# Weights from float64 by integer shifts and one integer addition, on VectorE, with the first batch's square sums

## The chip, the cores and the metric

The kernel runs on one core of one Trainium2 chip. A core has TensorE (PE: products, with a weight load PEld ahead of each), VectorE (DVE), ScalarE (ACT), GpSimd (POOL) and SyncE (SP, which issues the DMAs here). The metric is device time in microseconds of one execution, median over the timed runs.

## The reference

Channel attention over 6080 tokens of 256 channels, for four batches, then a gated two-layer product over all 24320 tokens:

```python
qn = q / (norm(q, axis=1) + 1e-06);  kn = k / (norm(k, axis=1) + 1e-06)
s = kn.transpose(0, 2, 1) @ qn / tau          # 4 x 256 x 256
a = softmax(s, axis=-1)
x = (v @ a).reshape(24320, 256)
h = x @ w_in                                  # 256 x 2048
out = (h * (1 / (1 + exp(-1.702 * h)))) @ w_out   # 2048 x 256
```

q, k and v are float32. The two weights come as float64 and have to be rounded to float32 on the chip, which has no float64 arithmetic: each word arrives as two 32-bit halves, low (`lw`) and high (`hw`).

## The kernel before

v (a w_in) is computed in place of (v a) w_in: a w_in is 256 x 2048 and is made once per batch (`weights`, L370, in four groups of 512 columns). float32 operands are split into two parts, hi by ScalarE (`split`, L78) and lo = x - hi by a subtraction on VectorE (L79), and a product is three products of parts.

The first batch's attention runs alone (L465 to L521), in an order written out by hand. Units of two tiles of 128 tokens pass through it: q and k are loaded four tiles at a time, ScalarE squares them (L238), and the squares are summed into `acc_q` and `acc_k` (L241), while TensorE makes the scores from the raw float32 words (L257), five units behind. There are 25 units; the last two are shorter. Of these sums GpSimd takes those of q in every second unit, as far as the last six units, and VectorE all others. After the last unit, both sums are folded (L287), and `norms_a` takes the norms: TensorE's products with ones (L288) give `ps_n`, VectorE copies it, and GpSimd takes the square root as a power (L296). `norms_b` makes reciprocals and a diagonal on VectorE, `norms_c` the product `ps_b` (L311) and its copy (L316), `softmax_a` and `softmax_c` the rows x (L329 to L347), `transposes` ends it. The scores of the last three units and some products of no use (`keep_warm`, L463) stand between these on TensorE.

The tokens then come in chunks of 512. For each chunk and each of 16 blocks of hidden units, a step: six products into `ps_h` (`hidden`, L419), a sigmoid on ScalarE (L425), the product g on VectorE (L426, one input from PSUM), its split into gh and gl, and two steps later six products into `ps_o` (`project`, L444). `ps_h` has three buffers. The first two chunks of the first batch alternate, so that each block of hidden units is needed every second step only. From L540 on, the order of each engine's instructions is chosen by a scheduler that keeps the program's dependences.

The weights are converted in 16 pieces of 128x512 words by `to_float32`: two while q and k come in (units 10 and 14, `spread` false), the others beside the first 24 steps (the table at L528), each begun at its step and carried on in the two that follow. A piece is loaded (`words`), ScalarE makes the absolute value of the high half into z (L119) and the low half times 2^-52 into m (L121), VectorE clamps z (L125), shifts it (L127), puts the sign back (L130) and cuts out the exponent (L134); GpSimd multiplies `low` with m (L136) and adds (L143). With `spread` false VectorE makes L124 and L138 in place of ScalarE's and GpSimd's parts. Pieces of w_in end in `win`, which is split group by group (`win_h`, `win_l`); pieces of w_out are split at once, `wo_h` by ScalarE, `wo_l` by GpSimd. z, `low` and the words of w_out have two buffers each.

The other three batches' attention goes in between the tokens of the batch ahead of it, with its square sums on GpSimd (`prepare`); the first begins at step 34.

Of the kernel before, what the change touches and what calls it, by code (L numbers as in the profile page):

```python
# [19 lines left out]
# high words of 2^128 and of 2^-127 in float64, their bits read as float32  # L20
F64_TOP = float(np.array([1151 << 20], np.uint32).view(np.float32)[0])
F64_BOTTOM = float(np.array([896 << 20], np.uint32).view(np.float32)[0])
NCH = 512  # tokens of one chunk
FG = 4  # blocks of 128 hidden units in one group of the first product's weights
# [3 lines left out]
def channel_attention_then_glu(  # L28
# [10 lines left out]
    """out = act((v a) w_in) w_out, with a = softmax(kn^T qn / tau) of one batch.  # L39

    (v a) w_in is taken as v (a w_in): a w_in is 256 x 2048 and made once per batch.
    float32 operands of products are split into two float32r parts, x = hi + lo
    exactly (12 significant bits each); hi hi + hi lo + lo hi leaves out only what
    lies below float32's own rounding of a product.

    The weights come as float64, of which the chip has no arithmetic: as their bits.
    They are rounded to float32 here.
    """
# [3 lines left out]
    NC2 = C // P  # halves of the channels  # L52
# [5 lines left out]
    T = N // P  # whole tiles of 128 tokens  # L58
    TAIL = N - T * P
    UT = 2  # tiles of one unit of the scores' loop  # L60
    RT = 4  # tiles of one load
# [15 lines left out]
    def split(dst_hi, dst_lo, src, eng=nc.vector):  # L77
        ins = nc.scalar.copy(dst_hi, src)  # L78
        eng.tensor_tensor(dst_lo, src, dst_hi.bitcast(F32), op=ALU.subtract)  # L79
        return ins  # L80

# [23 lines left out]
    def to_float32(out, raw, shape, spread):  # L105
        """float64 to float32: 2^e (1 + 20 bits of the high word), and below it the low
        word times 2^(e - 52), in one rounded sum. The high word without its sign is
        clamped to float32's exponents first, as a float32 itself, in which order its
        bits stand: what is too small comes out within 2^-126, too large as inf or NaN.
        spread: ScalarE and GpSimd take what they can of it. In parts, one for  # L110
        ScalarE, two for VectorE, one for GpSimd; it gives the result's tile."""
        lw = raw[..., 0]
        hw = raw[..., 1]
        z = cv.tile(shape, U32, tag="z", name="z")
        zf = z.bitcast(F32)
        low = cv.tile(shape, U32, tag="low", name="low")
        lf = low.bitcast(F32)
        if spread:
            nc.scalar.activation(zf, hw.bitcast(F32), AF.Abs)  # L119
            m = sp.tile(shape, F32, tag="sq", name="m", bufs=4)  # L120
            nc.scalar.activation(m, lw, AF.Copy, scale=2.0**-52)  # L121
        yield
        if not spread:
            nc.vector.tensor_single_scalar(z, hw, 0x7FFFFFFF, op=ALU.bitwise_and)  # L124
        nc.vector.tensor_scalar(zf, zf, F64_TOP, F64_BOTTOM, op0=ALU.min, op1=ALU.max)  # L125
        # exponent e - 896 in eight bits: the first of e's bits, then its last seven
        nc.vector.tensor_scalar(  # L127
            z, z, 5, 2, op0=ALU.logical_shift_left, op1=ALU.logical_shift_right
        )
        nc.vector.scalar_tensor_tensor(  # L130
            z, in0=hw, scalar=0xC0000000, in1=z, op0=ALU.bitwise_and, op1=ALU.bitwise_or
        )
        yield
        nc.vector.tensor_single_scalar(low, z, 0xFF800000, op=ALU.bitwise_and)  # L134
        if spread:
            nc.gpsimd.tensor_tensor(lf, lf, m, op=ALU.mult)  # L136
        else:
            nc.vector.scalar_tensor_tensor(  # L138
                lf, in0=lw, scalar=2.0**-52, in1=lf, op0=ALU.mult, op1=ALU.mult
            )  # L140
        yield
        out = zf if out is None else out
        nc.gpsimd.tensor_tensor(out, zf, lf, op=ALU.add)  # L143
        return out
# [3 lines left out]
    def win_fetch(n):  # L148
        """A block of 128 rows and GW columns; the words wait in the room of the next
        batch's q and k."""  # L150
        g, c = divmod(n, NC2)
        gs = slice(2 * g * GW, 2 * (g + 1) * GW)
        src = w_in[c * P : (c + 1) * P, gs].rearrange("p (f w) -> p f w", w=2)
        words["in", n] = load_words(src, [P, GW], sp, ("raw_q", "raw_k")[c])

    def win_convert(n, spread=True):
        g, c = divmod(n, NC2)
        out = win[:, c, g * GW : (g + 1) * GW]
        yield from to_float32(out, words.pop(("in", n)), [P, GW], spread)

    def wout_fetch(u):
        """Two blocks of 128 rows."""
# [4 lines left out]
    def wout_convert(u):  # L167
        t = yield from to_float32(None, words.pop(("out", u)), [P, 2, C], True)
        yield
        fs = slice(2 * u, 2 * u + 2)  # L170
        split(wo_h[:, fs, :], wo_l[:, fs, :], t, nc.gpsimd)
# [5 lines left out]
    class Attention:  # L177
        def __init__(self, b, direct=False):
            self.b = b
            # direct: float32 products, four passes each, with nothing to be split  # L180
            self.direct = direct
            self.raw = {}
            # tiles of each load: a short one first
# [3 lines left out]
            # (first tile, tiles, partitions) of each unit  # L187
# [4 lines left out]
        def load(self, t0, room):  # L192
            """Tiles t0 .. of q and k; a partition's rows are contiguous in DRAM."""
            b = self.b
            nt = min(room, T - t0)
            # the very first tiles come one by one
            cuts = range(nt + 1) if self.direct and t0 == 0 else (0, nt)
            tiles = {}
            for a, z in zip(cuts, cuts[1:]):
                for src, tag in ((q, "raw_q"), (k, "raw_k")):  # L200
                    if tag not in tiles:
                        if self.direct:  # the room of weights that are not there yet
# [14 lines left out]
        def prepare(self, u):  # L217
# [6 lines left out]
            else:  # L224
                # [hi | lo] side by side, so that one product takes both parts of q
# [4 lines left out]
            for r, nm in ((rq, "acc_q"), (rk, "acc_k")):  # L230
# [4 lines left out]
                else:  # L235
# [3 lines left out]
                    fast = self.direct and (nm == "acc_k" or u % 2 or u >= len(self.units) - 6)  # L239
                    eng = nc.vector if fast else nc.gpsimd  # L240
# [38 lines left out]
        def norms_a(self):  # L279
            """Columns: norms of both halves of q's channels, then of k's."""  # L280
# [26 lines left out]
        def norms_c(self):  # L307
            """1 / (q's norms) along the free axis, on all partitions."""
# [9 lines left out]
        def softmax_a(self):  # L318
# [19 lines left out]
            # the table of the function that follows comes in while the vector engine works  # L338
# [31 lines left out]
        def weights(self, g, i):  # L370
            """Half i of group g of a w_in."""
# [62 lines left out]
    def project(b, c, f, gh, gl):  # L434
        o, w = chunks[c]
        if f == 0:
            # the second chunk of all runs beside the first, in the room of the scores
# [20 lines left out]
    def keep_warm(rhs, n):  # L458
        """Products of no use, where the tensor engine would wait long enough for its
        clock to be halved: the next ones would run at half the rate."""  # L460
# [11 lines left out]
    with tc.manual_schedule():  # L472
        keep_warm(ones, 8)
        parts = []
        for u in range(nu):
# [7 lines left out]
            if u in early:  # L483
                parts.append(win_convert(early[u], False))
                next(parts[-1])
                next(parts[-1])
# [40 lines left out]
    # the weights' conversions, each begun at its step  # L527
# [116 lines left out]
```

## Time and profile before

| | |
|---|---|
| time, median of 3 runs | 2319.41 us (2319.32 to 2321.55) |
| span of the profiled execution | 2318.9 us |
| TensorE (PE) busy | 2295.2 us, 99%, 10300 records |
| VectorE (DVE) busy | 1397.3 us, 60% |
| ScalarE (ACT) busy | 1221.7 us, 53% |
| GpSimd (POOL) busy | 281.8 us, 12%, 207 records |

The times further below are us from the span's start, of the one profiled execution. The page gives no time of that execution beside its span. The shares are means over the whole span; the start of the kernel looks otherwise, and the rows below are of it. PEclk is the clock that TensorE was granted, as a share of 2.4 GHz. A record of an engine can begin before the one ahead of it has ended, by some 0.08 us on VectorE.

### The profile page before, as it was taken

How to read it: one execution, taken by the hardware profiler on the slowest of the kernel's cores; microseconds unless marked ns; L12 is line 12 of the kernel's file. 1: busy time of each engine (PE TensorE's matmuls, PEld its weight loads, DVE VectorE, ACT ScalarE, POOL GpSimd, SP SyncE). 2: the span in 40 equal slices, each digit the busy share in tenths (PEclk: the TensorE clock that was granted, in tenths of full speed). 3: DMA queues.
4: the chain of work that ended last, by engine and by line, in shares of the span. 5: the costliest groups of instructions: out<-in, count | busy, mean ns of one | idle time of the engine just before them, and what ended most of it. 6: DMA issues, size and time to landing. Idle time of an engine off the chain costs nothing.

```text
span 2318.9 us, 27421 instructions
## 1 busy us (share of the span) xinstructions
PE 2295.2 (99%) x10300; PEld 1909.0 (82%) x10300; DVE 1397.3 (60%) x2020; ACT 1221.7 (53%) x2104; POOL 281.8 (12%) x207
## 2 busy tenths in 40 slices
PE   8989999999999999999999999999999999999999
PEld 7768888888888888888888888888888888888888
DVE  7996666666565566566556656655555555555554
ACT  5665555555455555555455555554544444444444
POOL 3561222010030011110002002200000000000000
PEclk9999999999999999999999999999999999999999
DMA  7212121111021112111011112101000100000000
GB/s 297 82 55 82 64 61 67 35 37 36 19 72 37 55 55 72 36 37 36 19 37 54 55 37 73 55 26 37 18 19 20 35 18 26 30 19 25 30 10 18
DMA packets 46390, 109.77 MB, mean 47 GB/s; under 512 B 4528, under 2 KB 8624, under 8 KB 46256
## 3 DMA queue, kind: packets, MB, share of 16 engines
q1 hardware_dynamic: 46256, 108.02, 13.9%
q8 instruction: 80, 1.31, 0.2%
q14 instruction: 54, 0.44, 0.1%
HBM read 83.10 MB, written 24.90 MB: 47 GB/s over the span
## 4 chain that ended last, share of the span: by engine, by line
PE 94%; DVE 3%; issue 1%; DMA 1%; ACT 0%; POOL 0%; SPq 0%; DVEq 0%; ACTq 0%; POOLq 0%
PE ps_o L444 44%; PE ps_h L419 44%; PE s L262 3%; PE ps_w L384 2%; PE s L270 1%; DMA raw_k<-in_k 1%; DVE gl L79 1%; DVE z L130 0%; DVE g L426 0%; DVE z L125 0%; DVE z L127 0%; DVE acc_k L241 0%; DVE low L134 0%; PE s L257 0%; DVE acc_q L241 0%
## 5 line engine op out<-in xcount | busy, mean ns | idle before, releaser
L79 DVE TENSOR_TENSOR gl<-g,gh 128x512 fp32r<-128x512 f32 (+1 forms) x768 | 575.6, 751 | 387.1 <-ACT gh L78 381.8
L426 DVE TENSOR_TENSOR g<-ps_h,g 128x512 f32<-128x512 f32 (+1 forms) x768 | 523.7, 683 | 452.4 <-ACT g L425 448.7
L425 ACT ACTIVATE g<-ps_h 128x512 f32<-128x512 f32 (+1 forms) x768 | 453.6, 592 | 501.8 <-PE ps_h L419 495.8
L78 ACT CAST gh<-g 128x512 fp32r<-128x512 f32 (+1 forms) x768 | 472.5, 615 | 453.4 <-DVE g L426 339.5
L419 PE MATMUL ps_h<-v_h,wh 128*128 128x512 f32 (+1 forms) x1536 | 598.2, 390 | 3.7 <-DVE wl L79 3.0
L444 PE MATMUL ps_o<-gl,wo_h 128*128 128x512 f32 (+1 forms) x1536 | 596.6, 388 | 4.4 <-DVE gl L79 4.3
L419 PE MATMUL ps_h<-v_l,wh 128*128 128x512 f32 (+1 forms) x1536 | 596.3, 388 | 0.0
L419 PE MATMUL ps_h<-v_h,wl 128*128 128x512 f32 (+1 forms) x1536 | 595.8, 388 | 0.0
L444 PE MATMUL ps_o<-gh,wo_l 128*128 128x512 f32 (+1 forms) x1536 | 595.5, 388 | 0.0
L444 PE MATMUL ps_o<-gh,wo_h 128*128 128x512 f32 (+1 forms) x1536 | 504.2, 389 | 1.0 <-ACT wo_h L78 1.0
L444 PEld LDWEIGHTS ps_o<-gl,wo_h 128*128 128x128 f32 x1536 | 288.6, 188 | 64.2 <-DVE gl L79 7.4
L419 PEld LDWEIGHTS ps_h<-v_h,wh 128*128 128x128 f32 x1536 | 288.9, 188 | 63.1 <-DVE wl L79 3.4
L419 PEld LDWEIGHTS ps_h<-v_h,wl 128*128 128x128 f32 x1536 | 288.8, 188 | 58.4 <-DVE wl L79 0.2
L444 PEld LDWEIGHTS ps_o<-gh,wo_l 128*128 128x128 f32 x1536 | 288.6, 188 | 57.4
L419 PEld LDWEIGHTS ps_h<-v_l,wh 128*128 128x128 f32 x1536 | 289.0, 188 | 54.6
L444 PEld LDWEIGHTS ps_o<-gh,wo_h 128*128 128x128 f32 x1536 | 286.3, 188 | 57.8 <-ACT wo_h L78 1.4
L241 POOL TENSOR_TENSOR acc_q<-acc_q,sq 128x512 f32<-128x512 f32 (+1 forms) x81 | 108.0, 1333 | 1182.2 <-ACT sq L238 1021.9
L241 POOL TENSOR_TENSOR acc_k<-acc_k,sq 128x512 f32<-128x512 f32 (+1 forms) x72 | 109.3, 1518 | 4.0 <-ACT sq L238 3.8
L262 PE MATMUL s<-qs,ks 128*128 128x512 f32 (+1 forms) x288 | 109.1, 394 | 0.0
L238 ACT ACTIVATE sq<-raw_q 128x512 f32<-128x512 f32 (+1 forms) x96 | 58.3, 607 | 43.4 <-DMA raw_q<-in_q 35.1
L270 PE MATMUL s<-qs,ks 128*128 128x256 f32 (+1 forms) x288 | 80.8, 281 | 0.0
L79 DVE TENSOR_TENSOR v_l<-v_raw,v_h 128x1024 fp32r<-128x1024 f32 (+1 forms) x48 | 59.4, 1237 | 11.0 <-ACT v_h L78 9.5
(86 smaller groups left out, 1001.8 us busy)
## 6 DMA issues: line engine op xcount, KB each, us to landing
raw_q<-in_q SPq DMA_DIRECT2D x44, 512.0 KB, 3.9
raw_k<-in_k SPq DMA_DIRECT2D x44, 512.0 KB, 4.5
v_raw<-in_vT SPq DMA_DIRECT2D x44, 512.0 KB, 3.7
out_T<-osb SPq DMA_DIRECT2D x88, 256.0 KB, 2.1
words<-in_w_in SPq DMA_DIRECT2D x8, 512.0 KB, 7.5
words<-in_w_out SPq DMA_DIRECT2D x8, 512.0 KB, 3.4
v_raw<-in_vT SPq DMA_DIRECT2D x4, 448.0 KB, 3.5
out_T<-osb SPq DMA_DIRECT2D x8, 224.0 KB, 2.1
```

Source lines behind the costliest of these rows:

```text
L78: ins = nc.scalar.copy(dst_hi, src)
L79: eng.tensor_tensor(dst_lo, src, dst_hi.bitcast(F32), op=ALU.subtract)
L238: nc.scalar.activation(sq, r, AF.Square)
L241: eng.tensor_tensor(acc, acc, sq, op=ALU.add)
L262: nc.tensor.matmul(self.s[i], lhsT=ks[:pp, j, 0, ci], rhs=qs[:pp, j, :, :], start=first, stop=False, skip_group_check=True,)
L270: nc.tensor.matmul(self.s[i][:, C:], lhsT=ks[:pp, j, 1, ci], rhs=qs[:pp, j, 0, :], start=False, stop=last, skip_group_check=True,)
L384: nc.tensor.matmul(ps, lhsT=l[:, j, ci], rhs=r[:, j, :], start=n == 0, stop=n == 3 * NC2 - 1,)
L419: nc.tensor.matmul(ps[:, :w], lhsT=l[:, j, fs], rhs=r[:, j, :w], start=n == 0, stop=n == 3 * NC2 - 1,)
L425: newest[0] = nc.scalar.activation(g, ps[:, :w], AF.Sigmoid, scale=1.702)
L426: nc.vector.tensor_tensor(g, ps[:, :w], g, op=ALU.mult)
L444: nc.tensor.matmul(out[d][:, :w], lhsT=l[:, f, ds], rhs=r[:, :w], start=f == 0 and n == 0, stop=f == NF - 1 and n == 2,)
```

## The change

The two float64 halves are joined otherwise. The high half is clamped and shifted as before. The low half times 2^-29 is written by ScalarE as a whole number (its upper three bits, rounded; the buffer is named `eighths`), and an integer addition of z and `eighths` gives the float32's bits. That takes the place of the exponent's cut, the product and the float sum. All pieces go the same way: ScalarE's two steps are made for the two early pieces too, and what is left is on VectorE. The subtraction for `wo_l` and all of the first batch's square sums go to VectorE as well. The steps stand in another grouping: the shift ends a part, and the sign's step is a part of its own. Comments are gone, so the line numbers differ.

```diff
-    def split(dst_hi, dst_lo, src, eng=nc.vector):
+    def split(dst_hi, dst_lo, src):
         ins = nc.scalar.copy(dst_hi, src)
-        eng.tensor_tensor(dst_lo, src, dst_hi.bitcast(F32), op=ALU.subtract)
+        nc.vector.tensor_tensor(dst_lo, src, dst_hi.bitcast(F32), op=ALU.subtract)
...
-        low = cv.tile(shape, U32, tag="low", name="low")
-        lf = low.bitcast(F32)
-        if spread:
-            nc.scalar.activation(zf, hw.bitcast(F32), AF.Abs)
-            m = sp.tile(shape, F32, tag="sq", name="m", bufs=4)
-            nc.scalar.activation(m, lw, AF.Copy, scale=2.0**-52)
+        eighths = cv.tile(shape, U32, tag="low", name="eighths")
+        nc.scalar.activation(zf, hw.bitcast(F32), AF.Abs)
+        nc.scalar.activation(eighths, lw, AF.Copy, scale=2.0**-29)
         yield
-        if not spread:
-            nc.vector.tensor_single_scalar(z, hw, 0x7FFFFFFF, op=ALU.bitwise_and)
         nc.vector.tensor_scalar(zf, zf, F64_TOP, F64_BOTTOM, op0=ALU.min, op1=ALU.max)
         nc.vector.tensor_scalar(
             z, z, 5, 2, op0=ALU.logical_shift_left, op1=ALU.logical_shift_right
         )
+        yield
         nc.vector.scalar_tensor_tensor(
             z, in0=hw, scalar=0xC0000000, in1=z, op0=ALU.bitwise_and, op1=ALU.bitwise_or
         )
         yield
-        nc.vector.tensor_single_scalar(low, z, 0xFF800000, op=ALU.bitwise_and)
-        if spread:
-            nc.gpsimd.tensor_tensor(lf, lf, m, op=ALU.mult)
-        else:
-            nc.vector.scalar_tensor_tensor(
-                lf, in0=lw, scalar=2.0**-52, in1=lf, op0=ALU.mult, op1=ALU.mult
-            )
-        yield
         out = zf if out is None else out
-        nc.gpsimd.tensor_tensor(out, zf, lf, op=ALU.add)
+        nc.vector.tensor_tensor(out.bitcast(U32), z, eighths, op=ALU.add)
...
-        split(wo_h[:, fs, :], wo_l[:, fs, :], t, nc.gpsimd)
+        split(wo_h[:, fs, :], wo_l[:, fs, :], t)
...
-                    fast = self.direct and (nm == "acc_k" or u % 2 or u >= len(self.units) - 6)
-                    eng = nc.vector if fast else nc.gpsimd
+                    eng = nc.vector if self.direct else nc.gpsimd
...
-                parts.append(win_convert(early[u], False))
-                next(parts[-1])
+                parts.append(win_convert(early[u]))
                 next(parts[-1])
```

On VectorE, the first early piece stands among the square sums like this before (sums are L241, `acc_k` and `acc_q`):

```order
L124 TENSOR_SCALAR z<-words 128x512
L125 TENSOR_SCALAR z<-z 128x512
L127 TENSOR_SCALAR z<-z 128x512
L130 SCALAR_TENSOR_TENSOR z<-words,z 128x512
L241 TENSOR_TENSOR acc_q<-acc_q,sq 128x512
L241 TENSOR_TENSOR acc_k<-acc_k,sq 128x512
L134 TENSOR_SCALAR low<-z 128x512
L138 SCALAR_TENSOR_TENSOR low<-words,low 128x512
```

and like this in the change, behind the sums of unit 11 (sums are L229; L132 is the integer addition, which stands as 1024 parts of 16 bits):

```order
L121 TENSOR_SCALAR z<-z 128x512
L123 TENSOR_SCALAR z<-z 128x512
L229 TENSOR_TENSOR acc_q<-acc_q,sq 128x512
L229 TENSOR_TENSOR acc_k<-acc_k,sq 128x512
L127 SCALAR_TENSOR_TENSOR z<-words,z 128x512
L229 TENSOR_TENSOR acc_q<-acc_q,sq 128x512
L229 TENSOR_TENSOR acc_k<-acc_k,sq 128x512
L132 ISA win<-z,eighths 128x1024
```

A piece has four VectorE instructions in place of six, and each unit has both sums here.

GpSimd, from its first sum to the first piece of w_out, before:

```order
L241 TENSOR_TENSOR acc_q<-acc_q,sq 128x512 x6
L143 TENSOR_TENSOR win<-z,low 128x512
L241 TENSOR_TENSOR acc_q<-acc_q,sq 128x512 x2
L143 TENSOR_TENSOR win<-z,low 128x512
L241 TENSOR_TENSOR acc_q<-acc_q,sq 128x512
L296 TENSOR_TENSOR rn<-rn,half 128x4
L136 TENSOR_TENSOR low<-low,m 128x512
L143 TENSOR_TENSOR z<-z,low 128x512
L79 TENSOR_TENSOR wo_l<-z,wo_h 128x512
```

and in the change, where the sums behind the power are those of the second batch:

```order
masks.py:199 ISA
masks.py:199 AFFINE_SELECT ident<-ident 128x128
L284 TENSOR_TENSOR rn<-rn,half 128x4
L229 TENSOR_TENSOR acc_q<-acc_q,sq 128x512
L229 TENSOR_TENSOR acc_k<-acc_k,sq 128x512
```

GpSimd has only the power of the norms left until the second batch's sums.

VectorE at the first token steps, before (`wl` is the low part of a w_in, g and gl belong to steps, z and `low` to pieces):

```order
L79 TENSOR_TENSOR wl<-ps_w,wh 128x512 x2
L125 TENSOR_SCALAR z<-z 128x512
L127 TENSOR_SCALAR z<-z 128x512
L130 SCALAR_TENSOR_TENSOR z<-words,z 128x512
L426 TENSOR_TENSOR g<-ps_h,g 128x512
L134 TENSOR_SCALAR low<-z 128x512
L426 TENSOR_TENSOR g<-ps_h,g 128x512
```

and in the change:

```order
L79 TENSOR_TENSOR wl<-ps_w,wh 128x512 x2
L121 TENSOR_SCALAR z<-z 128x512
L123 TENSOR_SCALAR z<-z 128x512
L79 TENSOR_TENSOR wo_l<-z,wo_h 128x512
L127 SCALAR_TENSOR_TENSOR z<-words,z 128x512
L132 ISA win<-z,eighths 128x1024
L414 TENSOR_TENSOR g<-ps_h,g 128x512
```

The subtraction for `wo_l` and the integer addition stand ahead of the first g; the exponent's cut is gone.

## Rows read from the trace of the kernel before

**Rows 1.** Windows: stretch, length, busy PE PEld DVE ACT POOL, PEclk, DMA, GB/s.

```profile
20.50:51.40 30.90, 25.28 (x118) 21.93 (x117) 30.23 (x42) 19.90 (x36) 12.12 (x8) 0.95 0.91 347
51.40:68.10 16.70, 16.70 (x88) 14.62 (x89) 10.98 (x27) 6.84 (x13) 3.63 (x2) 0.79 0.21 64
68.10:154.80 86.70, 75.74 (x315) 57.58 (x314) 82.68 (x110) 56.15 (x101) 51.14 (x35) 0.99 0.26 80
154.80:170.00 15.20, 15.19 (x55) 12.12 (x56) 14.36 (x14) 8.14 (x15) 15.09 (x10) 0.80 0.00 0
170.00:2318.90 2148.90, 2144.06 (x9653) 1786.94 (x9651) 1249.34 (x1816) 1119.15 (x1926) 194.66 (x145) 1.00 0.12 39
```

**Rows 2.** Timeline of TensorE: start, duration, instruction, idle time ahead and its releaser.

```profile
8.96 36.56 PE L257 MATMUL s<-raw_q,raw_k 128*128 128x256 f32 x168 [1.19 <-DMA raw_k<-in_k]
51.14 1.01 PE L288 MATMUL ps_n<-ones,acc_q 128*128 128x1 f32 x4 [5.62 <-DVE acc_q L287]
...
52.87 5.47 PE L257 MATMUL s<-raw_q,raw_k 128*128 128x256 f32 x12
58.13 0.72 PE L311 MATMUL ps_b<-diag,ones 128*128 128x128 f32 x4
...
59.84 4.29 PE L463 MATMUL ps_x<-ones 128*128 128x128 f32 x36
63.96 0.60 PE L356 MATMUL ps_t<-ident,x 128*128 128x128 f32 x4
...
154.81 0.80 PE L419 MATMUL ps_h<-v_h,wh 128*128 128x512 f32 x1 [2.96 <-DVE wl L79]
```

**Rows 3.** Timeline of VectorE, first batch's squares to softmax.

```profile
25.64 0.43 DVE L127 TENSOR_SCALAR z<-z 128x512 uint32<-128x512 uint32 x1
26.10 0.69 DVE L130 SCALAR_TENSOR_TENSOR z<-words,z 128x512 uint32<-128x512 uint32 x1
26.71 0.68 DVE L241 TENSOR_TENSOR acc_q<-acc_q,sq 128x512 f32<-128x512 f32 x1
...
27.91 1.49 DVE L134 TENSOR_SCALAR low<-z 128x512 uint32<-128x512 uint32 x1
...
51.02 0.41 DVE L287 TENSOR_TENSOR acc_k<-acc_k 128x256 f32<-128x256 f32 x1
...
56.21 1.22 DVE L79 TENSOR_TENSOR v_l<-v_raw,v_h 128x1024 fp32r<-128x1024 f32 x1
...
59.52 0.48 DVE L329 SCALAR_TENSOR_TENSOR x<-s,rn,rq 128x256 f32<-128x256 f32 x1 [0.20 <-PE s L257]
...
62.75 0.62 DVE L347 TENSOR_SCALAR x<-x,z 128x256 f32<-128x256 f32 x2
```

**Rows 4.** Timeline of GpSimd beside them.

```profile
27.54 1.58 POOL L241 TENSOR_TENSOR acc_q<-acc_q,sq 128x512 f32<-128x512 f32 x1 [3.28 <-DVE acc_q L241]
```

**Rows 5.** VectorE by form, 68.1 to 156 us: busy, mean ns, idle ahead.

```profile
L79 DVE TENSOR_TENSOR gl<-g,gh 128x512 fp32r<-128x512 f32 x23 | 25.0, 1086 | 2.6 <-ACT gh L78 2.6
L426 DVE TENSOR_TENSOR g<-ps_h,g 128x512 f32<-128x512 f32 x23 | 15.6, 677 | 0.0
L130 DVE SCALAR_TENSOR_TENSOR z<-words,z 128x512 uint32<-128x512 uint32 x13 | 13.1, 1006 | 0.2
L127 DVE TENSOR_SCALAR z<-z 128x512 uint32<-128x512 uint32 x13 | 10.1, 777 | 0.2
L125 DVE TENSOR_SCALAR z<-z 128x512 f32<-128x512 f32 x13 | 10.1, 776 | 0.0
L134 DVE TENSOR_SCALAR low<-z 128x512 uint32<-128x512 uint32 x13 | 6.8, 526 | 0.1
...
L79 DVE TENSOR_TENSOR win_l<-win,win_h 128x1024 fp32r<-128x1024 f32 x3 | 4.7, 1579 | 0.0
```

**Rows 6.** Timeline of ScalarE: the second half of unit 11.

```profile
25.29 0.63 ACT L238 ACTIVATE sq<-raw_k 128x512 f32<-128x512 f32 x1 [0.66 <-DMA raw_k<-in_k]
```

**Rows 7.** Chain of waits: a piece in steady flow.

```profile
169.70 2.27 PE ps_o L444 x10
```

More of the change, by code (lines that the diff above doesn't have):

```diff
@@ L103, in load_words, with to_float32 @@
         return raw
-    def to_float32(out, raw, shape, spread):
+    def to_float32(out, raw, shape):
         lw = raw[..., 0]
@@ L154, in win_fetch, with win_convert @@
         words["in", n] = load_words(src, [P, GW], sp, ("raw_q", "raw_k")[c])
-    def win_convert(n, spread=True):
+    def win_convert(n):
         g, c = divmod(n, NC2)
         out = win[:, c, g * GW : (g + 1) * GW]
-        yield from to_float32(out, words.pop(("in", n)), [P, GW], spread)
+        yield from to_float32(out, words.pop(("in", n)), [P, GW])
     def wout_fetch(u):
@@ L167, in wout_convert @@
     def wout_convert(u):
-        t = yield from to_float32(None, words.pop(("out", u)), [P, 2, C], True)
+        t = yield from to_float32(None, words.pop(("out", u)), [P, 2, C])
         yield
         fs = slice(2 * u, 2 * u + 2)
-        split(wo_h[:, fs, :], wo_l[:, fs, :], t, nc.gpsimd)
+        split(wo_h[:, fs, :], wo_l[:, fs, :], t)
     fetch = {"in": win_fetch, "out": wout_fetch}
```

## The prediction, made before the change was run

> **What bounds the kernel now.** I read first the table of windows [rows 1]. From 170 us to the end TensorE is busy for 2144 of 2148.9 us at full clock, so nothing can be won or lost there, and whatever happens ahead of 170 us moves the end by the same amount. Ahead of it are four stretches: the first batch's squares and scores (to 51.4 us), its norms and softmax (to 68.1), the first tokens beside the weights' conversions (to 154.8), and a tail to 170. VectorE is busy for 30.2 of 30.9 us in the first and for 82.7 of 86.7 in the third; TensorE has gaps in both and a lower clock in the second and the fourth.
>
> Next the timeline of TensorE [rows 2]. Its scores end at 45.52 (8.96 + 36.56); then it stands 5.62 us until VectorE has added up the squares (L287), and norms start at 51.14. After that idle time the granted clock in the second stretch is 0.79 on average: a mix of 1.2 and 2.4 GHz. Twelve score records take 5.47 us there, against 12 x 0.218 = 2.6 us at the rate of the 168 before (36.56 / 168). A second wait, 2.96 us for VectorE's wl at 154.81, is again followed by a low clock, 0.80 in the fourth stretch.
>
> So VectorE sets the end of both stretches. Why it is so full is in the timelines of VectorE and GpSimd [rows 3, 4] and the table by form [rows 5]. L134 and L127 are the same kind of instruction on 128x512, yet L127 takes 0.43 us at 25.64 and L134 1.49 at 27.91, while GpSimd's add runs from 27.54 to 29.12. In the third stretch the gl subtraction, both inputs in SBUF, takes 1086 ns in the mean; the g product, of the same size with one input in PSUM, takes 677. VectorE's SBUF work stands still while GpSimd adds.
>
> **The change part by part.** *Squares and the two early conversions.* GpSimd's nine square sums and two sums of a conversion leave GpSimd until the norms; VectorE takes the nine sums. In each early conversion VectorE drops L124, L134 and L138 and gets one integer addition; ScalarE gets an Abs and a copy. Durations: a 128x512 step on two tensors takes 0.61 us from start to start (26.10 to 26.71), a scalar step followed by one that needs it 0.46 (25.64 to 26.10), a half-wide sum about 0.33 (0.41 less 0.08, by which neighbours' records overlap) [rows 3].
>
> The integer addition is not in this trace. From below it is the 0.61 us of a 128x512 sum, from above a 128x1024 one, 1.22 less 0.08 = 1.14 us (v_l, 56.21): in the order it stands as 1024 parts of 16 bits a row. I take 0.61, since z and eighths are 512 words. The Trainium skill ("VectorE: DVE Perf Modes", What auto-detection actually checks) has two-source instructions on adjacent 16-bit operands take two elements a cycle. By that rule it is 0.61, and without it 1.14, which is the first rival; no row shows it.
>
> ScalarE reads the second half of unit 11 (k) at 25.29, when it lands [rows 6], so its sum cannot start before 25.92. From there VectorE has, by its new order: 23 wide sums (unit 11's k, both of units 12 to 22) x 0.605 = 13.9; six half-wide ones x 0.33 = 2.0; two conversions x (0.46 + 0.46 + 0.61 + 0.61) = 4.3. That is 20.2 us, so 46.1 us instead of 51.4. Scores end at 45.5, thus TensorE's wait shrinks to some 0.5 us: cover and work are nearly level, and any longer VectorE work would show again. The four ScalarE activations hide in its 11 us of idle time in this stretch [rows 1]. The words' rooms come free with L127 and the eighths instead of L138, still ahead of the loads that follow at the end of the stretch, so SP's queue is not delayed.
>
> *Norms to softmax.* No instruction changes, only the start and the clock. If the clock stays at 2.4 GHz, the norm products behind the last sum take about 0.5 us (from 51.14 to 52.87 all of them take 1.7 at the lower clock, half of them wait for the last sum) [rows 2]: 46.6. From there to v_l it is 56.21 - 52.87 = 3.3 us [rows 2, 3], through GpSimd's power, which stays; so v_l starts at 49.9. The 12 scores now end by 46.6 + 2.6 = 49.2 instead of holding ps_b back until 58.13. v_l stands ahead of the copy of ps_b on VectorE, 1.14 us, and becomes the last: x starts at 51.3 (49.9 + 1.14 + a copy of about 0.3) instead of 59.52. x to the end of its last scaling (62.75 + 0.62 = 63.37) is 3.85 us, hence 55.15; the last score, with ps_b ahead of it, ends at about 51.2, and the filler products behind it take 63.96 - 59.84 = 4.1, hence 55.3 [rows 2, 3]. Transposes start there instead of at 63.96: 8.6 us earlier, taken as 8.5.
>
> *Token stage, 68.1 to 154.8.* TensorE's need: 315 records x 0.227 us (ten products take 2.27 in steady flow [rows 7]) = 71.5; so 15.2 of 86.7 us are lost. VectorE's need falls. Stretch that goes with GpSimd's sums, from the means less the clean durations [rows 3, 5] (the table by form runs to 156, two records further): gl 23 x (1.09 - 0.68) = 9.3, L130 13 x (1.01 - 0.69) = 4.1, L127 and L125 13 x 0.35 = 4.5 each, L134 13 x 0.10 = 1.3, win_l 3 x 0.36 = 1.1; sum 24.8. L134 itself goes: 13 x 0.35 = 4.5. It gets 13 integer additions x 0.61 = 7.9 and 7 wo_l subtractions x 0.61 = 4.3. 82.7 - 24.8 - 4.5 + 12.2 = 65.6 us, less than TensorE's 71.5. TensorE becomes the bound, with VectorE at 92% of its time. In-order queues at that load still miss each other; I leave a third of today's loss, 5 us. Gain 10. The bounds are 0 left (gain 15) and all left (0). ScalarE (56.2 of 86.7 us) loses nothing and gets nothing.
>
> *Tail.* 55 records x 0.227 = 12.5 of 15.2 us: 2.7 us, lost to the low clock behind the 2.96 us wait. With VectorE no longer late that wait goes; what is then late next is a gl or a wl by fractions of a us. Gain 2.7.
>
> Sum: 8.5 + 10 + 2.7 = 21.2. Against the profiled execution (span 2318.9, of which the page gives nothing but the span; the median of the timed runs is 0.5 above it) that is 2297.7, and 2298 for the median.
>
> **Rivals.**
> 1. *The addition takes one 16-bit part at a time*, 1.14 us. Squares end 2 x 0.53 = 1.1 us later. The token stage gets 13 x 0.53 = 6.9, VectorE's need is 72.5 against 71.5, and both are the bound: some 3 us more. 2302. For it: it writes 1024 elements, as v_l does. Against it: 512 words.
> 2. *The token stage is bound by latency, not by VectorE's load.* g, gh, gl pass through VectorE, ScalarE and VectorE again, with three score buffers; if half of the 15.2 us stays and the 2.7 too, the gain is 8.5 + 7.6 = 16 us, 2303; if all of it, 2311. For it: TensorE's need leaves VectorE only 8% slack. Against: today VectorE idles 2.6 us ahead of 23 gl and not at all ahead of 23 g [rows 5], so it is load that it lacks room for, not answers.
> 3. *Slower: VectorE's stretches are not GpSimd's doing.* Then the stretches stay and VectorE, the bound in both stages, simply gets more. First stretch: five of the nine sums fall behind 20.5 us (of GpSimd's 8 records [rows 1] two are conversions' and one began earlier), + 3.0, and two conversions lose 0.8 each, net + 1.4; token stage: + 7.9 - 4.5 + 4.3 = + 7.7. 2319.4 + 9 = 2328. Between 2328 with all of the stretch and 2298 with none, it decides once more than two thirds remain. Against it: stretched records begin and end with GpSimd's [rows 3, 4], the product out of PSUM is never stretched, and the half-wide sums at 51 us, GpSimd idle, are clean. The Trainium skill ("Perfetto Trace Analysis", Optimizing Scalar/DVE Operations) advises handing work off a full VectorE, to GpSimd even, which speaks against this change; it adds that the two share a read port, so that such moves may not help. By the first half alone the time would be this rival's 2328; the rows side with the second.
>
> **How the numbers follow.** Forecast 0.62 (2294 to 2302), rival 1 0.12 (around 2302), rival 2 0.17 (2302 to 2311), rival 3 0.03, and 0.06 for a time below 2294: all loss gone would be 2318.9 - 8.5 - 15.2 - 2.7 = 2292.5, plus 0.5. The range 2293 to 2307 holds the forecast, rival 1 and half of rival 2. Faster by over 0.2% (4.6 us, about what can be told from no change here) has 0.95: all but rival 3 and the far end of rival 2; 0.02 within it, 0.03 slower.
>
> **What would show it.** TensorE's wait ahead of the norms under 1 us instead of 5.6, no clock below 1.0 between 45 and 70 us, transposes near 55 us; gl at 0.68 to 0.75 us in the token stage and the addition's record at 0.69, or 1.22 by rival 1. Steady flow, without wait, reached about 21 us earlier. The prediction fails if VectorE's SBUF steps keep their 1 us means with GpSimd idle, or if TensorE still waits over 8 us in the token stage.

## The result and the profile after

The changed kernel takes 2298.12 us (median of 4 runs, 2298.09 to 2299.49) against 2320.43 us of the kernel before on the same chip (4 runs, 2319.32 to 2321.55): a ratio of 0.9907, 95% interval 0.9893 to 0.9921. The forecast was 2298. The profiled execution's span is 2296.3 us, 22.6 less than before.

The table of windows of the changed kernel, columns as in [rows 1]:

```profile
20.50:51.40 30.90, 30.59 (x146) 26.22 (x144) 27.71 (x53) 23.13 (x41) 1.93 (x1) 1.00 0.92 348
51.40:68.10 16.70, 16.15 (x93) 13.58 (x93) 14.75 (x32) 12.11 (x23) 0.00 (x0) 1.00 0.42 128
68.10:154.80 86.70, 84.06 (x366) 68.06 (x365) 77.02 (x123) 61.69 (x108) 14.84 (x8) 1.00 0.21 67
154.80:170.00 15.20, 15.20 (x69) 12.60 (x68) 9.60 (x14) 7.47 (x13) 0.00 (x0) 1.00 0.39 127
170.00:2296.30 2126.30, 2122.38 (x9558) 1770.53 (x9556) 1236.28 (x1797) 1108.10 (x1907) 194.79 (x145) 1.00 0.12 39
```

TensorE is nearly full and at full clock in every stretch: 84.06 of 86.7 us in the third, where it had 75.74. The same 86.7 us now hold 366 of its records instead of 315. VectorE has room in each stretch as a whole, though not everywhere in the third, as its waits below show.

TensorE's timeline, which answers to [rows 2]:

```profile
9.20 36.50 PE L245 MATMUL s<-raw_q,raw_k 128*128 128x256 f32 x168 [1.68 <-DMA raw_k<-in_k]
45.63 0.61 PE L276 MATMUL ps_n<-ones,acc_q 128*128 128x1 f32 x4
46.09 0.59 PE L276 MATMUL ps_n<-ones,acc_k 128*128 128x1 f32 x4
46.54 2.84 PE L245 MATMUL s<-raw_q,raw_k 128*128 128x256 f32 x12
...
55.51 0.60 PE L344 MATMUL ps_t<-ident,x 128*128 128x128 f32 x4
```

The 5.62 us ahead of the norms are gone, and twelve scores take 2.84 us instead of 5.47. Transposes start at 55.51, not 63.96: 8.45 us of the 22.6 are won by then, and 14.15 in the token stage and its tail.

VectorE's timeline, which answers to [rows 3] (L132 is the integer addition of the first early conversion):

```profile
30.38 0.68 DVE L132 CUSTOM_DVE_ANT_0 win<-z,eighths 128x1024 uint16<-128x1024 uint16 x1
30.98 0.68 DVE L229 TENSOR_TENSOR acc_q<-acc_q,sq 128x512 f32<-128x512 f32 x1
...
45.50 0.41 DVE L275 TENSOR_TENSOR acc_k<-acc_k 128x256 f32<-128x256 f32 x1
...
49.87 1.22 DVE L79 TENSOR_TENSOR v_l<-v_raw,v_h 128x1024 fp32r<-128x1024 f32 x1
...
51.54 0.48 DVE L317 SCALAR_TENSOR_TENSOR x<-s,rn,rq 128x256 f32<-128x256 f32 x1
```

The integer addition takes 0.68 us and the next step starts 0.60 behind it, like a float sum of 512 words.

VectorE by form, 60 to 136 us, which answers to [rows 5] (busy us, mean ns, idle ahead):

```profile
L79 DVE TENSOR_TENSOR gl<-g,gh 128x512 fp32r<-128x512 f32 x22 | 18.1, 834 | 0.9 <-ACT gh L78 0.7
L414 DVE TENSOR_TENSOR g<-ps_h,g 128x512 f32<-128x512 f32 x23 | 15.6, 683 | 3.0 <-ACT g L413 2.8
L127 DVE SCALAR_TENSOR_TENSOR z<-words,z 128x512 uint32<-128x512 uint32 x13 | 9.8, 751 | 0.0
L121 DVE TENSOR_SCALAR z<-z 128x512 f32<-128x512 f32 x13 | 6.4, 494 | 0.0
L123 DVE TENSOR_SCALAR z<-z 128x512 uint32<-128x512 uint32 x13 | 6.0, 459 | 0.1
```

gl is down from 1086 to 834 ns, the sign's step (L130 before, L127 now) from 1006 to 751, the clamp and the shift from about 777 to 494 and 459. They are not at the clean durations of 0.68 and 0.42 us yet. GpSimd's rows point to the reason: from the norms on it has nothing until 109 us, where the second batch's square sums begin.

```profile
46.97 1.93 POOL L284 TENSOR_TENSOR rn<-rn,half 128x4 f32<-128x4 f32 x1 [45.66 <-DVE rn L283]
109.24 1.29 POOL L229 TENSOR_TENSOR acc_q<-acc_q,sq 128x512 f32<-128x512 f32 x1 [60.35 <-ACT sq L227]
118.39 4.44 POOL L229 TENSOR_TENSOR acc_k<-acc_k,sq 128x512 f32<-128x512 f32 x1 [7.86 <-ACT sq L227]
```

In VectorE's table of the changed kernel from 60 to 100 us, GpSimd idle, everything is clean:

```profile
L79 DVE TENSOR_TENSOR gl<-g,gh 128x512 fp32r<-128x512 f32 x13 | 8.7, 683 | 0.1
L127 DVE SCALAR_TENSOR_TENSOR z<-words,z 128x512 uint32<-128x512 uint32 x8 | 5.4, 680 | 0.0
L123 DVE TENSOR_SCALAR z<-z 128x512 uint32<-128x512 uint32 x8 | 3.4, 420 | 0.1
L121 DVE TENSOR_SCALAR z<-z 128x512 f32<-128x512 f32 x8 | 3.3, 416 | 0.0
```

From 108 to 136 us, beside GpSimd's sums, it is not:

```profile
L79 DVE TENSOR_TENSOR gl<-g,gh 128x512 fp32r<-128x512 f32 x7 | 8.0, 1155 | 0.7 <-ACT gh L78 0.7
L127 DVE SCALAR_TENSOR_TENSOR z<-words,z 128x512 uint32<-128x512 uint32 x4 | 3.6, 909 | 0.0
```

In e12 (further below), where these sums are VectorE's and GpSimd is idle, gl takes 688 ns in the same window.

TensorE's waits in the changed kernel, 20 to 170 us (us in total, times, longest), come to 3.4 us, two of 0.3 among them that are left out here; before, they were 5.6 us ahead of the norms and 10.8 behind them:

```profile
PE ps_h L407 <- DVE wl L79: 1.6, 2, 1.4
PE ps_o L432 <- DVE gl L79: 1.2, 1, 1.2
...
```

These two, ahead of gl at 132.44 (1.25 us) and of wl at 136.62 (1.39), lie right at and behind the stretched steps. From 122.8 to 139.6 us VectorE is busy without a pause and TensorE for 14.17 of the 16.8 us, so all that TensorE still loses in the third stretch (2.6 us) is lost there.

### The profile page after: what moved, and what is told of

Same layout as the page of the kernel before. It is cut to its first block, busy times and chain, and to the rows that moved or that the text cites. A ratio compares the mean times of both kernels' runs of the same rounds, so it can differ in the third digit from the quotient of the medians.

```text
span 2296.3 us, 27390 instructions
## 1 busy us (share of the span) xinstructions
PE 2286.2 (100%) x10300; PEld 1906.7 (83%) x10300; DVE 1374.9 (60%) x2033; ACT 1224.0 (53%) x2108; POOL 212.3 (9%) x160
## 4 chain that ended last, share of the span: by engine, by line
PE 96%; issue 2%; DVE 1%; ACT 0%; POOL 0%; POOLq 0%; DVEq 0%; ACTq 0%
PE ps_o L432 45%; PE ps_h L407 45%; PE s L250 3%; PE ps_w L372 2%; PE s L258 2%; DVE gl L79 0%; PE ps_x L451 0%; DVE z L127 0%; DVE g L414 0%; PE ps_n L276 0%; PE ps_b L299 0%; POOL rn L284 0%; DVE wl L79 0%; PE ps_t L344 0%; DVE z L121 0%
## 5 line engine op out<-in xcount | busy, mean ns | idle before, releaser
L79 DVE TENSOR_TENSOR gl<-g,gh 128x512 fp32r<-128x512 f32 (+1 forms) x768 | 566.1, 739 | 383.2 <-ACT gh L78 379.1
L229 POOL TENSOR_TENSOR acc_q<-acc_q,sq 128x512 f32<-128x512 f32 (+1 forms) x72 | 93.8, 1303 | 1235.2 <-ACT sq L227 1082.8
L229 POOL TENSOR_TENSOR acc_k<-acc_k,sq 128x512 f32<-128x512 f32 (+1 forms) x72 | 112.2, 1558 | 11.1 <-ACT sq L227 10.8
```

The lines of the kernel that those rows point to most:

```text
L79: nc.vector.tensor_tensor(dst_lo, src, dst_hi.bitcast(F32), op=ALU.subtract)
L229: eng.tensor_tensor(acc, acc, sq, op=ALU.add)
```

## The experiments

Medians are of 4 runs unless said. The medians of the kernel before that were taken beside these kernels lie between 2319.76 and 2320.43 us, so differences of a few tenths of a us mean nothing. The table sets the start of the transposes beside the rest of the span from there, both of the profiled execution.

| kernel | time, us | transposes | from there to the end |
|---|---|---|---|
| before | 2320.28 (19 runs) | 63.96 | 2254.9 |
| changed | 2298.12 | 55.51 | 2240.8 |
| e1_squares | 2315.15 (10 runs) | 59.15 | 2253.6 |
| e2_squares_back | 2302.11 | 58.59 | 2241.1 |
| e3_float_on_vector | 2308.96 | 58.56 | 2248.1 |
| e4_warm_gap | 2317.78 (10 runs) | 60.84 | 2255.1 |
| e5_wo_l_back | 2301.69 | 55.69 | 2244.2 |
| e6_add_on_gpsimd | 2301.20 | 56.70 | 2241.4 |
| e7_gpsimd_adds | 2324.77 (1 run) | 63.23 | 2259.8 |
| e8_gpsimd_memsets | 2300.59 (1 run) | 56.18 | 2242.6 |
| e9_two_adds | 2303.11 | 56.55 | 2243.2 |
| e12_all_sums_again | 2295.07 | 55.31 | 2237.8 |

### The parts of the change by themselves

**e1_squares**: the kernel before, with only the first batch's square sums moved.

```diff
-                    fast = self.direct and (nm == "acc_k" or u % 2 or u >= len(self.units) - 6)
-                    eng = nc.vector if fast else nc.gpsimd
+                    eng = nc.vector if self.direct else nc.gpsimd
```

> The kernel before, with only the first batch's square sums all on VectorE; the conversions stay as they were, GpSimd's parts included. Theory (VectorE's steps on SBUF stand still while GpSimd adds): from 25.9 us VectorE has the changed kernel's 20.2 us, 1.6 more for the longer early conversions and up to 1.1 for each of GpSimd's two remaining sums, so the squares end at 47.5 to 50 us instead of 51.4 and TensorE's wait ahead of the norms shrinks from 5.6 to 2 to 4.5 us; the token stage stays as before. Time 2312 to 2318. Rival (the gain is the shorter conversion, and where the sums stand does not matter): VectorE gets five sums more behind 20 us, 3 us, squares end near 54, time about 2323.

Measured: ratio to before 0.998 (0.9971 to 0.9989). TensorE's timeline there:

```profile
48.16 0.61 PE L287 MATMUL ps_n<-ones,acc_q 128*128 128x1 f32 x4 [2.91 <-DVE acc_q L286]
```

VectorE takes nine sums more and is done 3 us earlier; TensorE's wait is nearly halved. The part behind the transposes is nearly as before (1.3 us shorter).

**e2_squares_back**: the changed kernel with GpSimd's nine sums put back (the lines above, the other way round).

> The changed kernel with GpSimd's nine square sums given back to GpSimd. Theory: each of the five sums behind 20 us takes 0.61 us off VectorE and stretches its neighbours by about 1.07 (1.76 less 0.68), so the squares end some 2.3 us later than 45.9, TensorE waits 2 to 3 us ahead of the norms; 2 to 3 us slower than the changed kernel, and 2 more if the clock falls behind that wait: 2300 to 2303. The token stage does not move. Rival (placement does not matter): VectorE is relieved by 3 us, the scores' end at 45.5 is the bound, time 2298 as it is.

Measured: ratio to before 0.9921 (0.9906 to 0.9936), 4.0 us slower than the changed kernel.

```profile
47.60 0.60 PE L277 MATMUL ps_n<-ones,acc_q 128*128 128x1 f32 x4 [1.92 <-DVE acc_q L276]
...
48.51 4.52 PE L246 MATMUL s<-raw_q,raw_k 128*128 128x256 f32 x12
```

Nearly all of the loss is ahead of the transposes (3.1 us of the span's 3.4). About 2.0 us of it is the wait, by which the norms start later; the rest is the clock behind it, at which the twelve scores take 4.52 us instead of 2.84.

**e3_float_on_vector**: the kernel before with its own float conversion, but with all of it, and the first batch's sums, on VectorE.

```diff
-            nc.gpsimd.tensor_tensor(lf, lf, m, op=ALU.mult)
+            nc.vector.tensor_tensor(lf, lf, m, op=ALU.mult)
...
-        nc.gpsimd.tensor_tensor(out, zf, lf, op=ALU.add)
+        nc.vector.tensor_tensor(out, zf, lf, op=ALU.add)
...
-        split(wo_h[:, fs, :], wo_l[:, fs, :], t, nc.gpsimd)
+        split(wo_h[:, fs, :], wo_l[:, fs, :], t)
```

> The kernel before with the same float arithmetic of the conversions (exponent cut, product, float sum), but every GpSimd step of the first batch moved to VectorE: squares, products, sums, low parts of w_out. It parts the placement from the shorter conversion. Theory: no stretch is left; an early conversion costs 1.4 us more than the changed kernel's, so squares end near 48.7; in the token stage VectorE needs 65.6 - 7.9 + 13 x (0.35 + 0.61 + 0.61) = 78 us against TensorE's 71.5 and is the bound: 4 to 8 us longer than the changed kernel's. Time 2304 to 2311. Rival (the gain is the integer form with fewer steps): VectorE's load only rises against the kernel before, 2320 or slower.

Measured: ratio to before 0.9952 (0.9936 to 0.9969). VectorE by form, 60 to 136 us, with GpSimd idle until 137:

```profile
L79 DVE TENSOR_TENSOR gl<-g,gh 128x512 fp32r<-128x512 f32 x21 | 14.3, 682 | 0.7 <-ACT gh L78 0.7
L130 DVE SCALAR_TENSOR_TENSOR z<-words,z 128x512 uint32<-128x512 uint32 x11 | 7.5, 683 | 0.0
L127 DVE TENSOR_SCALAR z<-z 128x512 uint32<-128x512 uint32 x12 | 5.0, 420 | 0.1
```

The same instructions, clean. VectorE does two steps more per piece, and a third for the pieces of w_out, and still gains: 6.8 us from the transposes to the end. It is as full as before (83.70 of 86.7 us, third stretch), now with work. The shorter integer way gives the other 7.3 us (2248.1 to 2240.8). Much of that is one place that the changed kernel does not have:

```profile
81.70 1.22 PE L383 MATMUL ps_w<-win_h,aT_h 128*128 128x512 f32 x2 [3.17 <-ACT win_h L78]
```

ScalarE stands 3.10 us ahead of that split until VectorE's float sum for `win` is done, and behind TensorE's wait the granted clock is 0.52 in 81 to 87 us.

**e4_warm_gap**: the kernel before, with 44 products of no use in TensorE's wait (`keep_warm(ones, 22)` ahead of `norms_a`), to keep the clock up.

> The kernel before with 22 products of no use (5.1 us) on TensorE in the gap between the scores and the norms; the wait for VectorE itself stays. It parts the clock from the wait. Theory: granted clock stays at 1.0 from 45 to 60 us, the 12 scores take 2.6 to 2.9 us instead of 5.47, transposes come at about 61 instead of 63.96; the gain is about 3 us: 2317. If the low clock cost nothing on the path: 2320.

Measured: ratio to before 0.999 (0.9981 to 0.9999), 2.5 us.

```profile
50.90 0.61 PE L288 MATMUL ps_n<-ones,acc_q 128*128 128x1 f32 x4 [0.72 <-DVE acc_q L287]
...
51.81 2.84 PE L257 MATMUL s<-raw_q,raw_k 128*128 128x256 f32 x12
```

The squares end as late as before, but the twelve scores take 2.84 us instead of 5.47 and the transposes are 3.1 us earlier. So of the 8.45 us ahead of the transposes about 3 were the low clock behind the wait, the rest the wait itself.

### Is it GpSimd that stretches VectorE?

**e5_wo_l_back**: the changed kernel with the eight subtractions for `wo_l` on GpSimd, as before.

```diff
-    def split(dst_hi, dst_lo, src):
+    def split(dst_hi, dst_lo, src, eng=nc.vector):
...
-        nc.vector.tensor_tensor(dst_lo, src, dst_hi.bitcast(F32), op=ALU.subtract)
+        eng.tensor_tensor(dst_lo, src, dst_hi.bitcast(F32), op=ALU.subtract)
...
-        split(wo_h[:, fs, :], wo_l[:, fs, :], t)
+        split(wo_h[:, fs, :], wo_l[:, fs, :], t, nc.gpsimd)
```

> The changed kernel with its eight wo_l subtractions back on GpSimd. Theory (a GpSimd step with two operands in SBUF costs VectorE more in stretched steps than the step itself would cost on VectorE): VectorE loses six steps of 0.60 us between 60 and 136 us and gains up to 1.07 us of stretch for each; 2298 to 2301 us, with the subtraction into gl above its 834 ns. Rival (a GpSimd step costs VectorE nothing, and what the change took from GpSimd was only late): VectorE is 3.6 us lighter and the time falls to 2295 to 2298 us, gl at 834 ns or less.

Measured: ratio to before 0.9922 (0.9905 to 0.9938), 3.6 us slower than the changed kernel, just above the theory's range. VectorE loses six steps and its gl grows to 937 ns:

```profile
L79 DVE TENSOR_TENSOR gl<-g,gh 128x512 fp32r<-128x512 f32 x22 | 20.5, 937 | 1.7 <-ACT gh L78 1.5
```

One late gl costs most of it. On TensorE's timeline:

```profile
138.82 0.50 PE L432 MATMUL ps_o<-gl,wo_h 128*128 128x512 f32 x1 [3.68 <-DVE gl L79]
```

Behind that wait the granted clock in 139 to 142 us is 0.68 on average.

**e6_add_on_gpsimd**: the changed kernel with the integer addition on GpSimd (`nc.vector` to `nc.gpsimd` in that line).

> The changed kernel with the integer addition of the conversion on GpSimd, 13 additions of 128x512 words, all else left. Theory (stretch): VectorE loses 13 steps of 0.60 us (7.8) and gains 13 stretches of about 1.07 us (14); the conversion is also later by the longer step ahead of the first weights; 2300 to 2305 us, gl at 1000 ns or more. Rival (VectorE is bound by its count of steps alone): 2293 to 2297 us. If GpSimd's integer addition takes much longer than the 1.2 to 1.7 us of its float sums, conversions come late to TensorE and its waits for weights show it.

Measured: ratio to before 0.9919 (0.9904 to 0.9934), 3.1 us slower than the changed kernel: in the theory's range, but not by its path. GpSimd's rows, 20 to 170 us:

```profile
L132 POOL TENSOR_TENSOR z<-z,eighths 128x512 uint32<-128x512 uint32 x8 | 13.0, 1627 | 30.2 <-DVE z L127 25.1 <-ACT win_h L78 3.5 <-ACT sq L227 1.6
L132 POOL TENSOR_TENSOR win<-z,eighths 128x512 uint32<-128x512 uint32 x8 | 11.6, 1452 | 56.6 <-DVE z L127 48.4 <-ACT sq L227 5.7 <-ACT gh L78 2.5
```

An addition takes 1.45 to 1.63 us there, 0.68 on VectorE. But gl's mean is 852 ns and not 1000: stretches fell on steps of less weight (`win_l` 1582 ns, `ks` 1776). Of the span's 1.8 us, 1.2 are lost ahead of the transposes, where the two early conversions' additions run beside the square sums (TensorE waits 1.0 us ahead of the norms). From the transposes on this execution loses 0.6 us. It is the fastest of the four, 1.3 us under their median, so the additions behind the transposes cost at most some 2 us more on GpSimd than on VectorE.

**e7_gpsimd_adds** and **e8_gpsimd_memsets**: the changed kernel with GpSimd work of no use behind the norms, first 28 additions that read SBUF, then 60 memsets that read nothing.

```diff
+        idle = op.tile([P, NCH], F32, tag="osb", name="idle")
+        for _ in range(28):
+            nc.gpsimd.tensor_tensor(idle, win[:, 0, :GW], win[:, 1, :GW], op=ALU.add)
```

> The changed kernel with 28 GpSimd additions of 128x512 float32 out of SBUF that nobody needs, from behind the square roots of the norms on (about 49 to 95 us). Theory (GpSimd steps on SBUF stretch VectorE's steps on SBUF): in 60 to 95 us the subtraction into gl and the conversion steps take 1.0 to 1.3 us instead of 0.5 to 0.83, the product g, which has an operand in PSUM, stays at 0.68; TensorE waits for gl and wl; 2304 to 2318 us. Rival (the stretches of the kernel before came from its own conversion steps, not from GpSimd): durations as in the changed kernel, 2298 us.

> The changed kernel with 60 GpSimd memsets of 128x512 float32 that nobody needs, at the place where the run before had 28 additions that read SBUF (span 2323.0 us, VectorE's shift-and-or step at 995 ns in 60 to 110 us, product g at 683). Theory (it takes GpSimd steps that read two operands in SBUF): VectorE's durations stay as in the changed kernel, 751 ns or less for that step; 2297 to 2300 us. Rival (any busy GpSimd stretches VectorE): 900 ns and more, and 2305 us or more.

Measured: 2324.77 and 2300.59 us, one run each; 26.7 and 2.5 above the changed kernel. With the additions the time lies above what the theory gave (2318 us at most), and so do the durations of all named steps but the clamp (1.3 us at most; the clamp takes 662 ns): the direction was right and the size too small. VectorE by form with the additions, 60 to 95 us:

```profile
L127 DVE SCALAR_TENSOR_TENSOR z<-words,z 128x512 uint32<-128x512 uint32 x4 | 5.9, 1464 | 0.0
...
L79 DVE TENSOR_TENSOR gl<-g,gh 128x512 fp32r<-128x512 f32 x3 | 5.2, 1760 | 0.0
L132 DVE CUSTOM_DVE_ANT_0 win<-z,eighths 128x1024 uint16<-128x1024 uint16 x2 | 3.4, 1706 | 0.0
L414 DVE TENSOR_TENSOR g<-ps_h,g 128x512 f32<-128x512 f32 x3 | 2.0, 678 | 0.0
```

and with the memsets, 60 to 100 us:

```profile
L414 DVE TENSOR_TENSOR g<-ps_h,g 128x512 f32<-128x512 f32 x13 | 8.8, 679 | 0.0
L79 DVE TENSOR_TENSOR gl<-g,gh 128x512 fp32r<-128x512 f32 x12 | 8.0, 680 | 0.7 <-ACT gh L78 0.7
L127 DVE SCALAR_TENSOR_TENSOR z<-words,z 128x512 uint32<-128x512 uint32 x7 | 4.7, 678 | 0.0
L121 DVE TENSOR_SCALAR z<-z 128x512 f32<-128x512 f32 x8 | 4.7, 585 | 0.0
L123 DVE TENSOR_SCALAR z<-z 128x512 uint32<-128x512 uint32 x7 | 4.6, 660 | 0.1
```

Additions of GpSimd stretch gl from 683 to 1760 ns, the sign's step from 680 to 1464 and the integer addition from 686 to 1706; the product out of PSUM stays at 678. Nothing else in the kernel is changed, so this shows the cause of the stretches by itself, and it falsifies the rival by which they came from the conversion's own steps. The 26.7 us are not all stretch. In this one execution the first loads came later (scores begin at 10.43 us, 9.20 in the changed kernel), and the norms start at 48.33 instead of 45.63, ahead of the first extra addition at 51.47: 2.7 of the 7.7 us ahead of the transposes are not the additions' doing. And TensorE's clock fell behind its waits (granted 0.57 in 54 to 62 us). Memsets leave every step with two inputs as it was, as expected; they do stretch the two scalar steps of one input (416 to 585 ns, 420 to 660), which was not expected. The time came out 0.6 us above the theory's range; whether these steps are why, one run does not tell.

The Trainium skill ("SBUF — State Buffer", Who interferes with whom) draws this very line: VectorE's steps in a two-port mode contend with GpSimd's, and a step with two SBUF inputs only with a GpSimd step that reads SBUF. The two traces agree, with 680 ns beside memsets and 1760 beside additions.

### How full VectorE may be, and a faster version

**e9_two_adds**: the changed kernel with each integer addition made twice on VectorE.

```diff
+        twice = op.tile(shape, U32, tag="osb", name="twice")
+        nc.vector.tensor_tensor(twice, z, eighths, op=ALU.add)
         nc.vector.tensor_tensor(out.bitcast(U32), z, eighths, op=ALU.add)
```

> The changed kernel with each of the 13 integer additions on VectorE made twice, the second into a buffer that nobody reads. Theory (VectorE's load bounds 60 to 136 us, with some 9 us of it idle): 7.8 us more of VectorE, half of it absorbed; 2300 to 2303 us. Rival (VectorE has room, and what is left of TensorE's waits is latency between engines): under 2299 us. The difference also bounds what an addition of twice the length would have cost: about 2302 us was forecast for that.

Measured: ratio to before 0.9927 (0.9912 to 0.9942), 5.0 us slower than the changed kernel and just above the theory's range. The profiled execution is the fastest of the four and shows 3.4 of them: ahead of the transposes 1.0 us is lost (1.2 us were added), behind them 2.4 (11 additions of 0.60 us, 6.6, were added), with VectorE at 83.90 of 86.7 us in the third stretch. So load on VectorE still had a price there, in that execution about a third of what is added.

**e10_all_sums_vector** and **e12_all_sums_again**: the changed kernel with the other batches' square sums and folds on VectorE too (the same kernel, measured twice), and **e11_after_again**, the changed kernel measured beside the second.

```diff
-                    eng = nc.vector if self.direct else nc.gpsimd
+                    eng = nc.vector
...
-                    eng = nc.vector if self.direct else nc.gpsimd
+                    eng = nc.vector
```

> The changed kernel with the second batch's square sums on VectorE too, so that GpSimd has no large step left. Between 109 and 134 us eight sums of about 0.60 us come to VectorE (4.8 us) and the stretches of that time go: gl from 834 to about 684 ns over 22 (3.3 us), the three conversion steps by some 2 us. Theory (a GpSimd sum costs VectorE about what it would cost on VectorE): no difference from the changed kernel within 1.5 us, 2297 to 2300 us. Rival (the end of stretches is worth more, since a wait of TensorE goes with it): below 2296 us. Rival (sums stand ahead of gl in VectorE's order, TensorE waits): above 2300 us.

> The changed kernel itself, beside the next one on the same chip. 2298 us, ratio 0.990 to 0.991. If the 2295.1 us of the version with all square sums on VectorE came from the chip and not from the kernel, this one is lower here as well.

> The version with all square sums on VectorE, of the run before, in more rounds. If the end of the stretches at 109 to 134 us is worth TensorE's waits that went (3.4 us in the changed kernel between 20 and 170 us, 0.8 in this one), it is 2 to 3 us below the changed kernel of the same call; if its four runs were low by chance, within 1 us of it.

Measured: 2295.12 (2294.77 to 2297.07) and 2295.07 us (2294.90 to 2296.25), ratios to before 0.9892 (0.9876 to 0.9909) and 0.9895 (0.9878 to 0.9911); the changed kernel beside the second 2297.85 (2297.70 to 2298.17), 0.9905 (0.9891 to 0.9920). The intervals of the ratios overlap. The runs do not: the slowest of the eight is 2297.07, the fastest of the changed kernel's eight 2297.70. The difference of the medians is 2.8 us, and my theory of "no difference within 1.5 us" fell to the first rival. The third row of e12's windows and two of TensorE's waits, 20 to 170 us:

```profile
68.10:154.80 86.70, 86.70 (x380) 71.06 (x380) 78.18 (x133) 63.47 (x111) 0.00 (x0) 1.00 0.22 73
```

```profile
...
PE ps_h L407 <- DVE g L414: 0.3, 1, 0.3
PE ps_h L407 <- DVE wl L79: 0.3, 1, 0.3
```

TensorE is busy for all of the third stretch, and its four waits are 0.3 us each. VectorE's work is not less (78.18 us against 77.02, with 14 records of TensorE more): eight sums cost 5.5 us, and the stretches that went were 5.8 (worked out below). That it still helps is put down to where the time falls: a stretch lengthens gl, which TensorE waits for, while a sum has slack. That reading fits the waits that went, but no run tests it by itself. It is the fastest version of this study.

## Why the prediction was right

**Squares.** The sums were to end at 46.1; the last fold ends at 45.91 (45.50 + 0.41). The wait ahead of the norms, forecast at 0.5 us, is nil. By the medians the nine sums alone are worth 5.1 us (e1) and 4.0 us (e2), a part of it by the clock. Between e1's transposes (59.15) and the changed kernel's (55.51) stand the two early conversions. e3 takes GpSimd's additions away from them and comes at 58.56, 0.6 us earlier; the shorter integer form gives the other 3.05: the folds end 1.9 us earlier (47.85 in e3), and the clock does not fall (twelve scores take 4.52 us in e3).

**The integer addition.** Taken at 0.61 us from start to start, measured 0.60. Rival 1 (one part of 16 bits at a time) is out. By the rule on adjacent 16-bit operands that the prediction set beside it (the Trainium skill, "VectorE: DVE Perf Modes", What auto-detection actually checks) two parts go per cycle, and the trace agrees: 1024 parts in 0.68 us, where 1024 words of float32 (v_l) take 1.22. From the time alone it cannot be told from 512 words at the rate of float32, which is how I had priced it. Rival 1's price, 2302, was about right: e9 pays an addition twice and takes 2303.1.

**Norms to softmax.** Norms done at 46.68 (46.6 forecast), v_l at 49.87 (49.9), x at 51.54 (51.3), transposes at 55.51 (55.3). The clock stayed up, and e4 shows that it was worth about 3 of the 8.45 us.

**Token stage and tail.** Forecast 12.7 us together, measured 14.15. Rival 2 needed half or all of TensorE's 15.2 us of loss to stay; 2.6 us stayed in the third stretch, where VectorE is busy without a pause, and none in the tail. e9 shows that load on VectorE has a price of its own. e3, which adds instructions, removes stretches and gains 6.8 us, does not part load from latency, since a clean gl is also an earlier one. Rival 3 is refuted by e3 and e7. The rows held against it were read a little too closely: L134 at 27.91 and GpSimd's sum at 27.54 overlap, but begin and end 0.3 to 0.4 us apart.

**How close the number came.** That 2298 met 2298.12 is luck. The sum of gains was 21.2 us and the span fell by 22.6. I added 0.5 us to get from the span to the time; in every run of which both are on record the time is 1.7 to 1.9 us above the span. The two errors, 1.4 and 1.3 us, cancel.

**What was mis-sized.** The sign "gl at 0.68 to 0.75 us in the token stage" did not come: it is 834 ns. VectorE's need in the third stretch was put at 65.6 us; it is 77.02. Two things were not in the sum. I took all 24.8 us of stretch away, but the second batch's sums, which stay on GpSimd, move into this stretch when everything comes earlier: gl 22 x (834 - 683) ns, L127 13 x (751 - 680), L121 13 x (494 - 416) and L123 13 x (459 - 420) are 5.8 us. And the stretch holds more work, as VectorE by form from 68.1 to 154.8 us shows:

```profile
L79 DVE TENSOR_TENSOR gl<-g,gh 128x512 fp32r<-128x512 f32 x30 | 23.6, 793 | 3.5 <-ACT gh L78 3.3
L414 DVE TENSOR_TENSOR g<-ps_h,g 128x512 f32<-128x512 f32 x28 | 19.0, 683 | 5.2 <-ACT g L413 5.0
```

These were 23 each [rows 5]: 12 steps more at 0.60 us from start to start are 7.2 us, splits of q, k and v beside them 2.3, while about two pieces of conversion (4.2 us) are done before it begins. 65.6 + 5.8 + 7.2 + 2.3 - 4.2 = 76.7. The first is a step that I left out: e12 takes those stretches away and gains 2.8 us. It did not show in the time because the 5 us of loss that I left over had no row behind them, and TensorE lost only 2.6 (86.70 less 84.06). That one guess covered what the other had missed is luck too.

## What to carry to other kernels

Before work is handed to GpSimd, look at what VectorE does beside it. Here VectorE's steps with both operands in SBUF were held up by GpSimd's steps that read SBUF (gl 1760 ns instead of 683 in e7), and a sum of 0.60 us on VectorE was cheaper than one of 1.3 us on GpSimd beside it (e1, e3, e12); for the integer additions behind the transposes it was nearer to even (e6). Compare the mean of one instruction form between stretches with GpSimd busy and idle; a busy engine may be full of waiting. And when a change pulls work forward, list what moves into the stretch that it shortens.

## What was not expected of the hardware

The hold-up goes both ways: GpSimd's sum at 118.39 us takes 4.44 us instead of 1.29, while VectorE runs steps with two SBUF inputs without a pause at their usual 0.68 us.

A memset of GpSimd (558 ns in the mean) leaves VectorE's two-input steps alone and stretches its one-input scalar steps by 0.17 to 0.24 us in the mean.

Waits of TensorE of 1.92 us (e2, ahead of the norms) and 3.68 us (e5) were followed by stretches at half clock (granted clock 0.73 on average in 47.6 to 51 us and 0.68 in 139 to 142); the 2.6 us of e9 and the 2.4 of e6, also for VectorE in the token stage, were not (1.00). So the length of a wait alone did not tell here whether the clock would fall.
